# First weight rows by one transfer each on two queues, ordered on VectorE while two more rows land

## The chip, the core and the metric

The kernel runs on one core of a Trainium2 chip. The core has a matrix engine (TensorE), a vector engine (VectorE), a scalar engine (ScalarE), GpSimd and SyncE, and transfers between main memory and the on-chip memory are issued by SyncE and by ScalarE, each through a queue of its own. In the profile these are PE (PEld for TensorE's weight loads), DVE, ACT, POOL and SP; "SPq" and "ACTq" are the instruction streams that issue transfers. The metric is the time of one execution in microseconds (us) on the device.

## What is computed

A weight matrix of 1024 x 1024 is pruned 2 of 4: along its first axis, each group of four consecutive rows keeps, in every column, the elements whose magnitude is at least the second largest of the four. Then 16 x 512 tokens of 1024 features are multiplied by the pruned matrix and a bias is added. All values are bfloat16.

```python
def reference(x, w, b):          # x 16 x 512 x 1024, w 1024 x 1024, b 1024
    B, S, D = x.shape
    N, M = 2, 4
    G = D // M
    wg = w.reshape(G, M, D)
    mag = jnp.abs(wg)
    order = jnp.argsort(mag, 1)
    thr = jnp.take_along_axis(mag, order[:, M - N:M - N + 1, :], 1)
    mask = (mag >= thr).astype(w.dtype)
    wp = (wg * mask).reshape(D, D)
    return jnp.einsum("bsd,df->bsf", x, wp) + b
```

## The kernel before

**Tiling.** The 8192 tokens are 64 tiles of 128. The output's 1024 columns are two halves of 512, one bank of accumulators each. The contraction over 1024 rows is eight steps of 128. A weight tile keeps one group of four rows on one partition: it is 128 partitions (groups) x 4 rows x columns. Two such tiles in the row direction (g = 0, 1) make the matrix.

**Pruning in pieces.** The matrix is pruned in six pieces (L61): four of g = 0, 256 columns wide, two of g = 1, 512 wide. For each, `abs_piece` (L109) takes magnitudes, on VectorE by masking the sign bit (L120) or for piece 3 on ScalarE (L117). `prep_piece` (L124) then forms, on VectorE, the larger (hi, L131) and smaller (lo, L132) of rows 0 and 1 and of rows 2 and 3, both pairs in one instruction; t1 and t2 (L135, L136); the threshold (L138), which is the second largest of the four; the mask (L145) and the product of weights and mask (L148). For piece 0 the magnitudes are taken in two instructions (rows 0 and 1, rows 2 and 3), and so are mask and product, rows 0 and 1 first.

**The start.** Transfers are issued at the top (L83 to L91), in program order on each queue. SyncE: rows 0 and 1 of piece 0's weights (128 KB), token tiles 0 and 1 (256 KB), tile 4 (128 KB), tile 5, the weights of piece 1 (256 KB), tiles 6 and 7, and the weights of pieces 2 and 3 (512 KB). ScalarE: rows 2 and 3 of piece 0's weights, tiles 2 and 3. Then ScalarE loads its function table and makes one small copy (L100). These token loads bring the first half of the features of tiles 0 to 7.

TensorE begins with filler matmuls on a constant (`warm`, L105, 13 of them, 12 before the first transposes; the profile holds records of 12), then transposes token tiles 0 to 3 (L175, four instructions a tile), one more filler, tiles 4 and 5. ScalarE copies each transposed tile out of its bank (L180). Then come the products (L196) of piece 0: for tiles 0, 1, 2 with rows 0 and 1, the same three tiles with rows 2 and 3, tile 3 with all four, tile 4 with rows 0 and 1, then the transposes of tiles 6 and 7 and what is left of piece 0 for the eight tiles; piece 1 follows. The whole order of the start is written out by hand in a string of tokens (`FRONT`), and every engine keeps program order.

**The rest.** Tiles 0 to 13 go through the weights as pieces become ready. Pruned weights are rearranged by transfers on SyncE (`unpack`, L165) into tiles with 128 rows of the contraction on the partitions, and later tokens are brought in already transposed, by transposing transfers on SyncE (L252, L264, L317). From tile 14 on, a loop does 16 matmuls a tile (L364), VectorE adds the bias (L241) and writes an output pair, two tiles to a buffer of 1024 columns each, five buffers in turn. The output of a pair leaves by one transfer of 512 KB on ScalarE's queue (L221), except for pairs in `singly` (L207), where each of the two tiles leaves by a transfer of its own (L214, L217). `singly` holds pairs 10 to 16, that is tiles 20 to 33.

Of the kernel before, what the change touches and what calls it, by code (L numbers as in the profile page):

```python
# [10 lines left out]
def kernel(  # L11
# [7 lines left out]
    nc = tc.nc  # L19
    P = 128  # L20
    bf16 = mybir.dt.bfloat16
    fp32 = mybir.dt.float32
    u16 = mybir.dt.uint16
    Alu = mybir.AluOpType
    Act = mybir.ActivationFunctionType
    K = tc.keep_in_program_order
# [6 lines left out]
    FH = 512  # L33
# [9 lines left out]
    tmp = ctx.enter_context(tc.tile_pool(name="tmp", bufs=2))  # L43
# [21 lines left out]
    def w_of(i):  # L65
        g, c0, c1 = pieces[i]
        return w_gh[(g, c0 // FH)][:, :, c0 % FH:c0 % FH + c1 - c0]

    def load_w(g, c0, c1, eng=nc.sync, m0=0, m1=4):
        dst = w_gh[(g, c0 // FH)][:, m0:m1, c0 % FH:c0 % FH + c1 - c0]  # L70
        K(eng.dma_start(dst, wv[:, g, m0:m1, c0:c1]))
# [4 lines left out]
    def load_x(ta, tb, eng=nc.sync):  # L76
        xt = const.tile([P, tb - ta, KH], bf16, name=f"xh_{ta}")
        src = xf[ta * P:tb * P, 0:KH].rearrange("(t p) c -> p t c", p=P)
        K(eng.dma_start(xt[:], src))
        for t in range(ta, tb):  # L80
            xh[t] = xt[:, t - ta, :]

    load_w(0, 0, 256, nc.sync, 0, 2)  # L83
    load_w(0, 0, 256, nc.scalar, 2, 4)
    load_x(0, 2)
    load_x(2, 4, nc.scalar)
    load_x(4, 5)
    load_x(5, 6)
    load_w(0, 256, 512)
    load_x(6, 8)  # L90
# [15 lines left out]

    mags = {}

    def abs_piece(i, on_act):  # L109
        g, c0, c1 = pieces[i]  # L110
        n = c1 - c0
        if n <= 256:
            mag = mags_pool.tile([P, 4, n], bf16, name="mag")[:]
        else:
            mag = mag2_pool.tile([P, 4, n], bf16, name="mag2")[:]
        if on_act:
            K(nc.scalar.activation(mag, w_of(i), Act.Abs))  # L117
        else:
            for ms in (slice(0, 2), slice(2, 4)) if i == 0 else (slice(0, 4),):
                K(nc.vector.tensor_single_scalar(  # L120
                    mag[:, ms].bitcast(u16), w_of(i)[:, ms].bitcast(u16), 0x7FFF, op=Alu.bitwise_and))
        mags[i] = mag

    def prep_piece(i):  # L124
        g, c0, c1 = pieces[i]
        n = c1 - c0
        mag = mags.pop(i)
        magv = mag.rearrange("p (a j) f -> p a j f", j=2)
        hi = tmp.tile([P, 2, FH], bf16, name="hi")[:, :, :n]
        lo = tmp.tile([P, 2, FH], bf16, name="lo")[:, :, :n]  # L130
        K(nc.vector.tensor_tensor(hi, magv[:, :, 0, :], magv[:, :, 1, :], op=Alu.max))  # L131
        K(nc.vector.tensor_tensor(lo, magv[:, :, 0, :], magv[:, :, 1, :], op=Alu.min))  # L132
        t1 = tmp.tile([P, FH], bf16, name="t1")[:, :n]
        t2 = tmp.tile([P, FH], bf16, name="t2")[:, :n]
        K(nc.vector.tensor_tensor(t1, hi[:, 0, :], hi[:, 1, :], op=Alu.min))  # L135
        K(nc.vector.tensor_tensor(t2, lo[:, 0, :], lo[:, 1, :], op=Alu.max))  # L136
        thr = tmp.tile([P, FH], bf16, name="thr")[:, :n]
        K(nc.vector.tensor_tensor(thr, t1, t2, op=Alu.max))  # L138
        mask = tmp.tile([P, 4, FH], bf16, name="mask")[:, :, :n]

        halves = (slice(0, 2), slice(2, 4)) if i < 3 else (slice(0, 4),)

        def keep(ms):
            tb = thr[:, None, :].to_broadcast([P, ms.stop - ms.start, n])
            K(nc.vector.tensor_tensor(mask[:, ms], mag[:, ms], tb, op=Alu.is_ge))  # L145

        def prune(ms):
            K(nc.vector.tensor_tensor(w_of(i)[:, ms], w_of(i)[:, ms], mask[:, ms], op=Alu.mult))  # L148

        if i == 0:  # L150
            for ms in halves:
                keep(ms)
                prune(ms)
        else:
            for ms in halves:
                keep(ms)
            for ms in halves:
                prune(ms)
# [45 lines left out]
            o_left[t // 2] = 2 if t == NT - 2 else 4  # L204
        return o_pair[t // 2][:, t % 2, :]

    singly = range(10, 17)  # L207

    def half_done(t):
        p = t // 2  # L210
# [82 lines left out]
    for tok in FRONT.split():  # L293
        k, *n = tok.split(".")
        n = [int(c) for c in n]
# [4 lines left out]
        elif k in "Ww":  # L300
            warm(FH if k == "W" else P)
        elif k == "A":
            abs_piece(n[0], n[0] == 3)
        elif k == "P":
            prep_piece(n[0])
        elif k == "T":
            transpose_half(n[0])
# [91 lines left out]
```

## Time and profile before

| | |
|---|---|
| runs (3), us | 233.02, 233.14, 233.35; median 233.14 |
| profiled execution, us | 233.16, of which 231.4 from first to last instruction |
| TensorE | 227.9 us busy, 98% |
| VectorE | 120.4 us busy, 52% |
| ScalarE | 18.0 us busy, 8% |
| main loop's matmuls (L364, 752 on the large token batches) | 162.5 us |
| piece products of g = 0 (L196, 256 columns, 128 of them) | 14.5 us |
| transposes on TensorE (L175) | 32 |

The queue streams at the start, with start and duration in us, the issuing engine, the line, the operation, what is written from what, and how many in a row:

```profile
0.73 0.46 SPq L71 DMA_DIRECT2D w<-in_w_dram  x1
0.74 0.49 ACTq L71 DMA_DIRECT2D w<-in_w_dram  x1
1.25 1.43 SPq L79 DMA_DIRECT2D xh<-in_x_dram  x3
1.26 0.50 ACTq L79 DMA_DIRECT2D xh<-in_x_dram  x1
1.79 1.28 ACT L100 ACT_TABLE_LOAD   x1 [1.79 <-issue]
2.73 0.68 SPq L71 DMA_DIRECT2D w<-in_w_dram  x1
3.44 0.61 SPq L79 DMA_DIRECT2D xh<-in_x_dram  x1
4.10 1.24 SPq L71 DMA_DIRECT2D w<-in_w_dram  x2
```

The duration of an issue is the time on the issuing engine only; how long a transfer takes to land stands in the view of transfers ("us to landing"). Lines of the list of waits read: who waited, for whom, us in total, times, the longest. In the timeline the bracket tells how long the engine was idle before and what ended that. Matmul durations in the profile overlap each other, so TensorE's pace is read from starts, not from durations.

### The profile page before, as it was taken

What the parts mean: (1) busy time and instruction counts of PE and PEld (TensorE: products, weight loads), DVE (VectorE), ACT (ScalarE), POOL (GpSimd) and SP (SyncE); (2) the same over time, 40 slices, a digit from 0 to 9 for tenths busy, and PEclk for the clock granted to TensorE, in tenths of its full rate; (3) what the DMA queues carried; (4) which work ended last, traced back from release to release, by engine and by line L of the source; (5) the groups of instructions that cost most, each with busy time, mean ns of one, the idle gap of its engine ahead of it and who ended that gap; (6) DMA issues with size and microseconds to landing.
All of it is one profiled execution on the core that took longest, in us unless ns stands there. A gap on an engine that the chain in (4) does not pass through costs nothing.

```text
span 231.4 us, 2786 instructions
## 1 busy us (share of the span) xinstructions
PE 227.9 (98%) x1156; PEld 110.8 (48%) x1156; DVE 120.4 (52%) x208; ACT 18.0 (8%) x33; POOL 0.7 (0%) x6
## 2 busy tenths in 40 slices
PE   8999999999999999999999999999999999999995
PEld 4887444444444444444444444444444444444443
DVE  3899887867987424424424424423423433433434
ACT  3777500000000000000000000000000000000000
POOL 1000000000000000000000000000000000000000
PEclk9999999999999999999999999999999999999999
DMA  6989998999957222991259622696129961122222
GB/s 208 264 179 233 218 192 177 267 258 270 320 189 272 91 95 70 235 284 58 81 129 251 164 93 92 137 241 192 68 91 200 224 211 40 53 91 91 91 93 91
DMA packets 77100, 38.19 MB, mean 165 GB/s; under 512 B 63136, under 2 KB 68896, under 8 KB 77088
## 3 DMA queue, kind: packets, MB, share of 16 engines
q1 hardware_dynamic: 67712, 20.91, 44.5%
q10 hardware_dynamic: 9376, 17.11, 20.4%
q8 instruction: 9, 0.15, 0.3%
q14 instruction: 3, 0.02, 0.0%
HBM read 3.41 MB, written 16.78 MB: 87 GB/s over the span
## 4 chain that ended last, share of the span: by engine, by line
PE 98%; DVE 0%; issue 0%
PE bank L364 73%; PE bank L196 17%; PE bank L256 6%; PE bank L105 2%; PE bank L175 1%; DVE o_last L347 0%
## 5 line engine op out<-in xcount | busy, mean ns | idle before, releaser
L364 PE MATMUL bank<-wp_nat,xTb 128*128 128x512 bf16 x752 | 162.5, 379 | 0.0
L241 DVE TENSOR_TENSOR o_pair<-bank,bias_sb 128x512 bf16<-128x512 f32 x104 | 67.3, 686 | 99.5 <-PE bank L364 96.3
L364 PEld LDWEIGHTS <-xTb 128*128 128x128 bf16 x752 | 73.6, 98 | 88.7
L232 DVE TENSOR_TENSOR stage<-bank,stage 128x512 f32<-128x512 f32 x22 | 14.4, 687 | 3.4 <-PE bank L196 3.3
L196 PE MATMUL bank<-w,xT 128*128 128x256 bf16 x128 | 14.5, 273 | 0.0
L196 PE MATMUL bank<-wp_nat,xg 128*128 128x512 bf16 x64 | 14.1, 379 | 0.0
L236 DVE TENSOR_TENSOR o_pair<-stage,bias_sb 128x512 bf16<-128x512 f32 x22 | 14.0, 683 | 0.0
L196 PEld LDWEIGHTS <-xT 128*128 128x128 bf16 x128 | 12.2, 98 | 1.8 <-ACT xT L180 0.2
L228 ACT COPY stage<-bank 128x512 f32<-128x512 f32 x22 | 11.4, 611 | 3.7 <-PE bank L196 3.7
L196 PE MATMUL bank<-wp_nat,xfill 128*128 128x512 bf16 x48 | 10.7, 379 | 0.0
L256 PE MATMUL bank<-wp_nat,xfill 128*128 128x512 bf16 x48 | 10.5, 379 | 0.0
L196 PEld LDWEIGHTS <-xg 128*128 128x128 bf16 x64 | 6.3, 98 | 7.5
L256 PEld LDWEIGHTS <-xfill 128*128 128x128 bf16 x48 | 4.7, 97 | 5.7
L196 PEld LDWEIGHTS <-xfill 128*128 128x128 bf16 x48 | 4.7, 98 | 5.4
L364 PE MATMUL bank<-wp_nat,xTs 128*128 128x512 bf16 x32 | 7.1, 379 | 0.0
L145 DVE TENSOR_TENSOR mask<-mag,thr 128x512 bf16<-128x512 bf16 (+2 forms) x9 | 5.5, 630 | 0.2
L148 DVE TENSOR_TENSOR w<-w,mask 128x512 bf16<-128x512 bf16 (+2 forms) x9 | 5.5, 630 | 0.2
L105 PE MATMUL bank<-const-bfloat16-1.0 128*128 128x512 bf16 (+1 forms) x12 | 4.4, 542 | 0.8 <-PEq L383 0.8
L364 PEld LDWEIGHTS <-xTs 128*128 128x128 bf16 x32 | 3.1, 98 | 3.8
L120 DVE TENSOR_SCALAR mag<-w 128x512 uint16<-128x512 uint16 (+2 forms) x6 | 2.7, 468 | 3.1 <-DMA w<-in_w_dram 3.1
L180 ACT COPY xT<-bank 128x512 bf16<-128x512 bf16 x8 | 4.1, 607 | 2.8 <-PE bank L175 2.8
L256 PE MATMUL bank<-wp_nat,xTb 128*128 128x64 bf16 (+3 forms) x40 | 3.7, 251 | 0.0
(20 smaller groups left out, 26.4 us busy)
## 6 DMA issues: line engine op xcount, KB each, us to landing
out_dram<-o_pair ACTq DMA_DIRECT2D x24, 512.0 KB, 2.8
out_dram<-o_pair ACTq DMA_DIRECT2D x15, 256.0 KB, 2.1
wp_nat<-w SPq DMA_DIRECT2D x16, 128.0 KB, 2.9
w<-in_w_dram SPq DMA_DIRECT2D x3, 512.0 KB, 6.9
xh<-in_x_dram SPq DMA_DIRECT2D x2, 256.0 KB, 4.4
xh<-in_x_dram ACTq DMA_DIRECT2D x1, 256.0 KB, 4.0
xh<-in_x_dram SPq DMA_DIRECT2D x2, 128.0 KB, 3.9
w<-in_w_dram SPq DMA_DIRECT2D x1, 256.0 KB, 4.2
```

What stands on the lines that cost most here:

```text
L105: K(nc.tensor.matmul(bank[7][:, :n], lhsT=ones[:, :P], rhs=ones[:, :n], start=True, stop=True))
L120: K(nc.vector.tensor_single_scalar(mag[:, ms].bitcast(u16), w_of(i)[:, ms].bitcast(u16), 0x7FFF, op=Alu.bitwise_and))
L145: K(nc.vector.tensor_tensor(mask[:, ms], mag[:, ms], tb, op=Alu.is_ge))
L148: K(nc.vector.tensor_tensor(w_of(i)[:, ms], w_of(i)[:, ms], mask[:, ms], op=Alu.mult))
L180: K(nc.scalar.copy(xt[:], src))
L196: K(nc.tensor.matmul(dst, lhsT=lhs, rhs=rhs, start=c0 == 0 and m == 0, stop=c1 == FH and m == 3))
L228: K(nc.scalar.copy(stage[(h, t)][:], bank[own[(h, t)]][:]))
L232: K(nc.vector.tensor_tensor(st, bank[own[(2 + h, t)]][:], st, op=Alu.add))
L236: K(nc.vector.tensor_tensor(get_o(t)[:, f], stage.pop((h, t))[:], bias_sb[:, f], op=Alu.add))
L241: K(nc.vector.tensor_tensor(get_o(t)[:, f], bank[bk][:], bias_sb[:, f], op=Alu.add))
L256: K(nc.tensor.matmul(bank[bk][:, :c1 - c0], lhsT=xN[t][:, kt, :], rhs=wp_nat[h][:, kt, c0:c1], start=kt == 0, stop=kt == KT - 1))
L364: K(nc.tensor.matmul(bank[bks[h]][:], lhsT=xN[t][:, kt, :], rhs=wp_nat[h][:, kt, :], start=kt == 0, stop=kt == KT - 1))
```

## The change

Four things are edited.

- The weights of rows 0 and 1 of piece 0 come by two transfers of 64 KB, row 0 on SyncE's queue and row 1 on ScalarE's, both first on their queues. Rows 2 and 3 (128 KB) are second on SyncE's queue.
- Token tiles 0 and 1 move from SyncE's queue to ScalarE's, tiles 2 and 3 from ScalarE's to SyncE's, tile 4 from SyncE's to ScalarE's.
- For piece 0, hi and lo of a pair of rows are formed directly after that pair's magnitudes, so that VectorE's order is abs, hi, lo of rows 0 and 1, then abs, hi, lo of rows 2 and 3, each hi and lo 256 columns wide instead of 2 x 256. For the other pieces the instructions are as they were.
- `singly` starts at pair 11: the outputs of tiles 20 and 21 leave by one transfer.

```diff
-    load_w(0, 0, 256, nc.sync, 0, 2)
-    load_w(0, 0, 256, nc.scalar, 2, 4)
-    load_x(0, 2)
-    load_x(2, 4, nc.scalar)
-    load_x(4, 5)
+    load_w(0, 0, 256, nc.sync, 0, 1)
+    load_w(0, 0, 256, nc.scalar, 1, 2)
+    load_w(0, 0, 256, nc.sync, 2, 4)
+    load_x(0, 2, nc.scalar)
+    load_x(2, 4)
+    load_x(4, 5, nc.scalar)
     load_x(5, 6)
     load_w(0, 256, 512)
     load_x(6, 8)
...
+    pairs = {}
+
+    def order_pairs(i, mag, a):
+        n = mag.shape[-1]
+        if i not in pairs:
+            pairs[i] = (tmp.tile([P, 2, FH], bf16, name="hi")[:, :, :n], tmp.tile([P, 2, FH], bf16, name="lo")[:, :, :n])
+        magv = mag.rearrange("p (a j) f -> p a j f", j=2)
+        for dst, op in zip(pairs[i], (Alu.max, Alu.min)):
+            K(nc.vector.tensor_tensor(dst[:, a], magv[:, a, 0, :], magv[:, a, 1, :], op=op))
...
-            for ms in (slice(0, 2), slice(2, 4)) if i == 0 else (slice(0, 4),):
+            for a in ((0, 1), (1, 2)) if i == 0 else ((0, 2),):
+                ms = slice(2 * a[0], 2 * a[1])
                 K(nc.vector.tensor_single_scalar(
                     mag[:, ms].bitcast(u16), w_of(i)[:, ms].bitcast(u16), 0x7FFF, op=Alu.bitwise_and))
+                if i == 0:
+                    order_pairs(i, mag, slice(*a))
...
-        magv = mag.rearrange("p (a j) f -> p a j f", j=2)
-        hi = tmp.tile([P, 2, FH], bf16, name="hi")[:, :, :n]
-        lo = tmp.tile([P, 2, FH], bf16, name="lo")[:, :, :n]
-        K(nc.vector.tensor_tensor(hi, magv[:, :, 0, :], magv[:, :, 1, :], op=Alu.max))
-        K(nc.vector.tensor_tensor(lo, magv[:, :, 0, :], magv[:, :, 1, :], op=Alu.min))
+        if i > 0:
+            order_pairs(i, mag, slice(0, 2))
+        hi, lo = pairs.pop(i)
...
-    singly = range(10, 17)
+    singly = range(11, 17)
```

## The prediction, made before the changed kernel had run

> **What bounds the kernel now.** I read the head of the page and its chain of waits first. TensorE is busy for nearly the whole span, and the chain that ends last is TensorE alone.
>
> ```profile
> span 231.4 us, 2786 instructions
> PE 227.9 (98%) x1156; PEld 110.8 (48%) x1156; DVE 120.4 (52%) x208; ACT 18.0 (8%) x33; POOL 0.7 (0%) x6
> PE 98%; DVE 0%; issue 0%
> ```
>
> So the end moves only if TensorE's first 11 us move. Next I read the chain in order of time there, the list of waits, and single instructions in narrow timeline windows.
>
> ```profile
> 0.77 4.21 PE bank L105 x11
> 4.99 1.20 PE bank L175 x16
> ...
> 6.68 2.15 PE bank L196 x18
> 8.84 0.51 PE bank L175 x8
> 9.35 36.21 PE bank L196 x222
> ```
>
> ```profile
> PEld L196 <- ACT xT L180: 0.2, 1, 0.2
> PEld L175 <- DMA xh<-in_x_dram: 0.2, 1, 0.2
> ```
>
> Filler matmuls (L105) run to 4.78, tokens are transposed (L175), and then the products start (L196). The narrow windows show where TensorE waits after 4.78, against matmuls that follow each other in 0.055 us (128 columns) or 0.109 (256): 0.05 at 6.57 (rows 0 and 1 pruned), 0.06 at 7.07 (third copied token tile), 0.07 at 7.37 (rows 2 and 3 pruned), 0.07 around 8.71 (tokens 6 and 7 land), 0.02 at 10.29. In all 0.27 us, 0.12% of the span: no shorter wait at the front can bring more. The fillers also stay, so nothing can start before 4.78.
>
> The third reading is VectorE in its timeline and the transfers by their issue windows.
>
> ```profile
> 3.55 0.53 DVE L120 TENSOR_SCALAR mag<-w 128x512 uint16<-128x512 uint16 x2 [2.68 <-DMA w<-in_w_dram]
> 4.11 0.43 DVE L131 TENSOR_TENSOR hi<-mag 128x512 bf16<-128x512 bf16 x1
> 4.45 0.42 DVE L132 TENSOR_TENSOR lo<-mag 128x512 bf16<-128x512 bf16 x1
> 4.79 0.29 DVE L135 TENSOR_TENSOR t<-hi 128x256 bf16<-128x256 bf16 x1
> 4.99 0.28 DVE L136 TENSOR_TENSOR t<-lo 128x256 bf16<-128x256 bf16 x1
> ```
>
> ```profile
> w<-in_w_dram SPq DMA_DIRECT2D x1, 128.0 KB, 2.8
> w<-in_w_dram ACTq DMA_DIRECT2D x1, 128.0 KB, 3.0
> ...
> xh<-in_x_dram SPq DMA_DIRECT2D x1, 256.0 KB, 3.5
> xh<-in_x_dram ACTq DMA_DIRECT2D x1, 256.0 KB, 4.0
> ```
>
> Issued at 0.73 and 0.74, the two weight halves land at 3.53 and 3.74. Tokens 0 and 1 (SyncE's queue, issued 1.25) land at 4.75, just as the fillers end; tokens 2 and 3 (ScalarE's, 1.26) at 5.26, and are wanted at 5.52.
>
> **The first weight rows.** Rows 0 and 1 become two transfers of 64 KB, and 128 KB fewer lie in front of them. The two queues together move 256 GB/s between 1.9 and 3.3 and about 350 at the end of that stretch, so 128 KB are worth 0.37 to 0.5 us against the later half's 3.74. Bounds for the landing: 3.25 to 3.74 (no gain, if the fixed part of the 3.0 us rules). I take 3.40, nearer the gain, since the bytes ahead are halved in any case.
>
> The Trainium skill speaks against this step: the page "DMA: Bandwidth & Descriptors", section "Issuing engines are not separate DMA queues", says that transfers from several engines share the same DMA engines and that only issue time is saved. The two rows above (2.8 and 3.0 us side by side) agree in that neither queue has the wires to itself. If only that rule counted and the landing stayed at 3.74, the sum below would end 0.35 us later.
>
> **VectorE's share.** The row 3.55 to 4.79 is the old stretch from first weights to t: two abs, one hi, one lo, 1.24 us. The new one has six instructions: abs, hi, lo, abs, hi, lo. The spacings: abs to a hi that needs it 0.33 (the second abs at 3.78 to 4.11); 256-column tensor operations 0.20 apart (4.79 to 4.99). So 0.33 + 0.20 + 0.20 for each half, 1.46 us with no wait. From 3.42 that puts t at 4.88, 0.09 later than 4.79. It breaks even with a landing at 3.31. Rows 2 and 3 must be there when the second abs wants them, at 4.15. They are now second on SyncE's queue beside tokens 0 and 1: no earlier than 3.74 (the same 256 KB end then), and, if all 256 KB of tokens slip in between at 350 GB/s, as late as 4.5. I take 3.95, covered by 0.2 us of VectorE's own work. With that cover gone each further 0.1 costs 0.1. t therefore comes between 4.73 and 5.22, 4.88 taken.
>
> What is queued behind on VectorE: the threshold, masks and products of piece 0, then all of piece 1. TensorE's start at 6.57 and 7.37 goes 0.09 later; 0.035 of that is given back at 8.71, where it waits for tokens 6 and 7 until 8.67 anyway. Piece 1's last product ends at 10.64 and is wanted at 10.74, so a delay of the same 0.05 passes there too. At 11.04 VectorE waits for the next weights by DMA (0.40 us idle), and later pieces are as before. Cost: 0.05 us.
>
> **Tokens 0 and 1 on ScalarE's queue.** Second on that queue, with 64 KB ahead. Between SyncE's 4.75 and ScalarE's old 5.26; the 64 KB that are gone from ahead are 0.2 us at 350 GB/s, so not over 5.06. I take 4.85, 0.10 late, keeping 4.6 (no use, the fillers run) to 5.26. Late by d, the copies on ScalarE (L180, 0.48 apart, the bound until 7.07) start d later; of d, 0.07 is given back where rows 2 and 3 are waited for and 0.035 at 8.71. So 0.10 costs nothing beyond VectorE's 0.05, the two overlapping. Tokens 2 and 3 on SyncE's queue behind more bytes: 5.0 to 5.5, wanted at 5.52, cost 0. Token tile 4 goes from SyncE to ScalarE, wanted at 6.02 with 0.33 us to spare, cost 0; tile 5 stays on SyncE with 64 KB less ahead. ScalarE issues three transfers instead of two, 0.50 each, so its table load ends at 3.58 instead of 3.08; its next work is at 5.45, which hides it. SyncE issues as many before the weights of piece 1 as before (four), so those and tokens 6 and 7 leave at 2.73 and 3.44 again.
>
> **What is not moved but comes near.** Tokens 6 and 7 took 5.2 us from 3.44 and end on the path: bounds -0.2 to +0.5 us (from nothing to the 0.5 that the two queues differ by above). I take 0: they leave at the same time with the same bytes ahead. One more transfer at the front costs its issue on ScalarE, priced above; if SyncE must besides wait for an early landing before it issues so many, the early ones are down by 4 and the large weights leave at 4.10, so that lies within the same upper bound.
>
> **The outputs of tokens 20 and 21.** Two transfers of 256 KB (81.23 and 84.69, 2.1 us each) become one of 512 KB at 84.69, 2.8 us by the paired rows, so it ends at 87.5; SyncE's next transposing load is issued at 90.48 and the output buffer is wanted five pairs later. Cost 0; with that cover gone, 0.7.
>
> **The sum.** +0.05 (VectorE) + 0 (tokens) + 0.02 for one instruction that waits on two landings (half of the 0.05 between a product's end at 7.32 and TensorE's start at 7.37): +0.07 on the profiled execution's own 233.16 (span 231.4 and 1.8 around it), 233.23; the runs' median is 233.14, 0.02 below it, so 233.2.
>
> **Rivals.** (a) First tokens late: on ScalarE's queue they land as that queue's row did, at 5.26 or after. TensorE idles 0.5 us, ScalarE's copies go with it, 0.10 is given back: +0.4, 233.55. For: the row itself. Against: half the bytes ahead. From a landing of 5.35 on it is over 0.2%. Chance 0.15.
>
> (b) Slow TensorE lasts longer. Until 5.5 matmuls start 0.427 apart for 512 columns, later 0.216: the clock doubles after 4.7 us of work. If an empty stretch at 4.78 made that count begin anew, 4.5 us more would run at half speed, +2.2, less the 0.27 of waits that vanish: 235.1. Against: the array is full for the whole 4 us before. Chance 0.08. The Trainium skill, "TensorE: Matmul & The Clock Gate", Part 1, ties the step to a free-running window of 3.4 us of activity; by it the estimate is half of 3.4 us later, less the same waits, 234.6; that page alone has the window, one clock step is all this trace shows.
>
> (c) A tail of the DMA queue: tokens 6 and 7, or the weights of 11.04 (piece 2's pruning ends 0.05 before it is used at 14.2), land 0.5 late because the queues' shares changed. Each 0.1 costs 0.1: 233.7. For: no slack at either. Against: the same bytes lie ahead. Chance 0.12.
>
> (d) Faster: row landings before 3.3, and the waits at 6.57, 7.37 and 8.71 vanish: -0.1 to -0.27, 232.95. Against: needs three landings better at once. Chance 0.13.
>
> (e) The change does not bring the first rows earlier (3.7): VectorE 0.4 late, +0.35; it is the upper end of my forecast, chance 0.52 for that whole case.
>
> **How the numbers follow.** A measurement of this kernel tells 0.2%, 0.47 us. Slower by more: all of (b), half of (a) and of (c), and 0.04 of the forecast's tail, together 0.25. Faster by more needs more than all waits of the front, that is, an earlier clock step: 0.05. The rest, 0.70, is within. Range 233.0 to 233.8: left out are (b), half of (d) and the far end of (c).
>
> **What would show it.** VectorE's first abs near 3.4 and t near 4.9; the first transposes at 4.78 to 4.95; products from 6.6; tokens 6 and 7 again near 8.7; from 11 us on every TensorE start shifted by one constant, under 0.2. An idle TensorE at 4.8 shows (a); 512-column starts or transposes at half speed after 5.5 show (b). The prediction is wrong if a wait after 11 us appears, or if the shift is over 0.4 either way.

## The result, and the profile after

| | before | changed |
|---|---|---|
| median, us | 233.22 (232.86 to 233.88, 12 runs) | 233.63 (233.55 to 233.97, 12 runs) |
| ratio | | 1.0020, 95% interval 1.0011 to 1.0029 |
| profiled execution, us | 233.16 (span 231.4) | 233.62 (span 231.8) |

The changed kernel is slower by 0.2%, some 0.4 to 0.5 us. The head of the page and the chain that ended last, of the changed kernel:

```profile
span 231.8 us, 2769 instructions
PE 227.1 (98%) x1137; PEld 110.9 (48%) x1156; DVE 120.7 (52%) x210; ACT 18.1 (8%) x33; POOL 0.7 (0%) x6
PE 95%; DMA 2%; issue 1%; DVE 0%; SPq 0%
```

Before, the chain was TensorE alone; now 2% of it is a transfer. The same chain in order of time (start, us, what):

```profile
1.19 0.42 SPq L71
1.65 4.55 DMA xh<-in_x_dram
6.24 0.64 PE bank L187 x8
6.94 0.45 PE bank L187 x8
7.38 1.97 PE bank L208 x18
9.35 0.45 PE bank L187 x8
```

The load of token tiles 2 and 3, issued on SyncE's queue at 1.65, takes 4.55 us; only at 6.20 are they there, and TensorE's third transposed tile starts at 6.24. Before, it started at 5.57 (its weight load at 5.52). The same load was issued at 1.26 before, as the second on ScalarE's queue; now it is the third on SyncE's and its issue starts 0.39 us later. The transfers by their issue windows (KB each, us from issue to landing; the one with 5.3 is the weights of piece 1):

```profile
w<-in_w_dram ACTq DMA_DIRECT2D x1, 64.0 KB, 2.3
w<-in_w_dram SPq DMA_DIRECT2D x1, 64.0 KB, 2.1
...
xh<-in_x_dram ACTq DMA_DIRECT2D x1, 256.0 KB, 3.8
w<-in_w_dram SPq DMA_DIRECT2D x1, 128.0 KB, 2.8
...
xh<-in_x_dram SPq DMA_DIRECT2D x1, 256.0 KB, 4.5
xh<-in_x_dram ACTq DMA_DIRECT2D x1, 128.0 KB, 4.4
...
w<-in_w_dram SPq DMA_DIRECT2D x1, 256.0 KB, 5.3
```

Rows 0 and 1 land at 2.83 and 3.00 (3.53 for both together before), rows 2 and 3 at 3.95 (3.76), tiles 0 and 1 at 4.95 (4.74), tiles 2 and 3 at 6.20 (5.24), the weights of piece 1 at 7.93 (6.91), tiles 6 and 7 at 8.62 (8.67). So the first rows come early, and two loads behind them, tiles 2 and 3 and the weights of piece 1, come a microsecond late. Tiles 4 and 5 come 0.4 later too (6.07 and 6.47, before 5.69 and 6.07). VectorE and TensorE in the timeline:

```profile
3.02 0.29 DVE L132 TENSOR_SCALAR mag<-w 128x512 uint16<-128x512 uint16 x1 [2.15 <-DMA w<-in_w_dram]
...
4.71 0.28 DVE L147 TENSOR_TENSOR t<-hi 128x256 bf16<-128x256 bf16 x1
...
6.24 0.64 PE L187 MATMUL bank<-ident,xh 128*128 128x128 bf16 x8 [0.21 <-DMA xh<-in_x_dram]
...
7.22 2.13 PE L208 MATMUL bank<-w,xT 128*128 128x256 bf16 x18
7.96 0.43 DVE L132 TENSOR_SCALAR mag<-w 128x1024 uint16<-128x1024 uint16 x1 [0.71 <-DMA w<-in_w_dram]
```

VectorE reaches t at 4.71 instead of 4.79, and the pruned rows 0 and 1 are there at 6.45. TensorE's first product starts at 7.22 instead of 6.57, 0.65 later: it waits for nothing on VectorE any more. Of the 0.65, 0.20 is given back, since the waits of before at 7.07, 7.37 and 8.71 no longer arise. From the first product behind the transposes of tiles 6 and 7 (9.63, before 9.19) to the end of the span TensorE is shifted by one constant, 0.45 us within 0.01. VectorE sits idle 0.71 us until the weights of piece 1 land, but the first product of piece 1 starts at 11.19, no more than the same 0.45 after the 10.74 of before.

### The profile page after: what moved, and what is told of

Its sections match the earlier page's. It is cut to its first block, busy times and chain, and to the rows that moved or that the text cites. A ratio compares the mean times of both kernels' runs of the same rounds, so it can differ in the third digit from the quotient of the medians.

```text
span 231.8 us, 2769 instructions
## 1 busy us (share of the span) xinstructions
PE 227.1 (98%) x1137; PEld 110.9 (48%) x1156; DVE 120.7 (52%) x210; ACT 18.1 (8%) x33; POOL 0.7 (0%) x6
## 4 chain that ended last, share of the span: by engine, by line
PE 95%; DMA 2%; issue 1%; DVE 0%; SPq 0%
PE bank L376 73%; PE bank L208 16%; PE bank L268 6%; DMA xh<-in_x_dram 2%; PE bank L187 1%; DVE o_last L359 0%; SPq L71 0%; PE bank L106 0%
```

## The experiments

Each kernel was timed against the kernel before on the same chip. "Ratio" is to that, with its 95% interval. Landing times are read from a single trace each.

**The changed kernel once more.** No edit.

> The changed kernel once more, for a second trace. Token theory (TensorE waits until tiles 2 and 3 land on SyncE's queue, 6.2 us in the first trace against 5.2 before): the landing comes again at 6.0 to 6.3, TensorE's third transposed tile starts right behind it, and the time is 233.5 to 233.8. Clock theory (the later doubling of TensorE's clock, at 5.96 us instead of 5.49, is what costs): the doubling is again near 5.96 whenever the time is 0.4 up; if it comes at another moment, the time follows it by half of the difference. Chance theory (one late landing in one execution): tiles 2 and 3 land at 5.3 to 5.6 this time and the time is 233.2.

233.81 us, ratio 1.0028 (1.0017 to 1.0038). TensorE in the timeline of the second trace:

```profile
0.77 3.65 PE L106 MATMUL bank<-const-bfloat16-1.0 128*128 128x512 bf16 x11 [0.77 <-PEq L395]
5.25 0.64 PE L187 MATMUL bank<-ident,xh 128*128 128x128 bf16 x8 [0.84 <-DMA xh<-in_x_dram]
6.33 0.64 PE L187 MATMUL bank<-ident,xh 128*128 128x128 bf16 x8 [0.44 <-DMA xh<-in_x_dram]
```

Tiles 2 and 3 land at 6.28 again: the late landing is no chance. The clock theory falls. The eleven fillers ahead of the transposes took 3.65 us in this trace and 4.21 in the first, because TensorE's pace doubled at 3.7 us here and at 5.96 there, and the profiled executions still took 233.72 and 233.62.

**The outputs of tiles 20 and 21 singly.** Edit on the changed kernel:

```diff
-    singly = range(11, 17)
+    singly = range(10, 17)
```

> The outputs of tiles 20 and 21 by a transfer each again, all else as in the changed kernel. All theories of the start: no change against the changed kernel, 233.6 within 0.1. Output theory (the joined transfer of 512 KB costs): 233.2 to 233.4.

233.88 us, ratio 1.0027 (1.0016 to 1.0037), as the changed kernel beside it. The joined output costs nothing that can be seen; tiles 2 and 3 landed at 6.11 in this trace too.

**VectorE's new order alone.** The kernel before with `order_pairs` for piece 0, all transfers and `singly` as before.

> The kernel before with VectorE's new order alone (six instructions for piece 0 instead of four), all transfers as before. VectorE theory: first weights at 3.53, t at 5.0 instead of 4.79, rows 2 and 3 pruned 0.2 later, of which 0.04 is given back at tokens 6 and 7: 233.3, +0.15. If VectorE's first piece does not bind: 233.15, within 0.05 of before.

233.26 us against 233.09, ratio 1.0003 (0.9994 to 1.0011): no difference. In this trace the two weight halves landed at 3.26 and 3.47, and t started at 4.76, 1.48 us after the first abs could start: the six instructions take what was worked out. Only the first landing differs from the 3.53 that was assumed.

**VectorE's old order on the new transfers.** Edit on the changed kernel:

```diff
-                if i == 0:
-                    order_pairs(i, mag, slice(*a))
...
-        if i > 0:
-            order_pairs(i, mag, slice(0, 2))
+        order_pairs(i, mag, slice(0, 2))
```

> The changed kernel with VectorE's order of before for piece 0 (both abs, then one hi and one lo over both pairs); transfers as in the changed kernel. Arithmetic from the changed kernel's trace: second abs at 3.97, hi at 4.30, lo at 4.64, t at 4.98 instead of 4.71. Wait theory (TensorE waits for tiles 2 and 3 until 6.24, the first product is at 7.2, the pruned rows are there at 6.5): no change against the changed kernel, 233.6 to 233.8. VectorE theory: +0.2, 233.9.

233.75 us, ratio 1.0031 (1.0020 to 1.0042). t starts at 5.34 instead of the 4.98 worked out, for rows 2 and 3 landed at 4.31 this time. Tiles 2 and 3 landed at 5.94, and the first product is at 7.13, directly behind VectorE. The time isn't told apart from the changed kernel's: VectorE's order has little or no weight while tiles 2 and 3 land this late.

**Swapping the token tiles alone.** Edit on the kernel before:

```diff
-    load_x(0, 2)
-    load_x(2, 4, nc.scalar)
+    load_x(0, 2, nc.scalar)
+    load_x(2, 4)
```

> The kernel before with token tiles 0 and 1 on ScalarE's queue and tiles 2 and 3 on SyncE's, nothing else (tile 4 stays on SyncE's). Token theory by queue: each pair lands as its queue's row did before, tiles 0 and 1 at 5.25, tiles 2 and 3 at 4.75; TensorE begins its transposes at 5.3, 0.5 late, and gives 0.1 back: 233.5, +0.4. If the queue does not matter, only the order of issue: tiles 0 and 1 at 4.8 and no change, 233.15.

233.53 us, ratio 1.0019 (1.0010 to 1.0028). The list of waits and TensorE's timeline:

```profile
PEld L175 <- DMA xh<-in_x_dram: 0.7, 1, 0.7
```

```profile
5.44 1.14 PE L175 MATMUL bank<-ident,xh 128*128 128x128 bf16 x16 [0.46 <-DMA xh<-in_x_dram]
```

As the theory by queue said: tiles 0 and 1 land at 5.39 on ScalarE's queue, tiles 2 and 3 at 4.94 on SyncE's. With equal transfers ahead of both, ScalarE's queue is the later one by 0.5 us (before: 4.74 and 5.24, the other way round).

**Token tiles back, weight rows split.** Edit on the changed kernel:

```diff
-    load_x(0, 2, nc.scalar)
-    load_x(2, 4)
-    load_x(4, 5, nc.scalar)
+    load_x(0, 2)
+    load_x(2, 4, nc.scalar)
+    load_x(4, 5)
```

> Token tiles on their old queues (0, 1 and 4 on SyncE's, 2 and 3 on ScalarE's), the weight rows and VectorE's new order as in the changed kernel. Token theory: tiles 2 and 3 land by 5.3, the wait before the third transposed tile is gone; tiles 0 and 1, now behind two weight transfers on SyncE's queue, land at 4.9 to 5.2, and the time is 233.2 to 233.4, at least 0.2 under the changed kernel. Clock theory: no change against the changed kernel, 233.6, as long as TensorE has an empty stretch at 4.8. Rows theory (the three weight transfers at the head push everything behind them back): 233.6, with tiles 0 and 1 after 5.3.

233.79 us, ratio 1.0026 (1.0016 to 1.0037): no gain. The wait has moved. Tiles 2 and 3, second on ScalarE's queue, land at 4.70; tiles 0 and 1, now third on SyncE's, at 5.42; and tiles 6 and 7, with one more load ahead of them on SyncE's queue and issued 0.4 later, at 9.33 instead of 8.67, which TensorE waits for.

**Weight rows back, token tiles swapped.** Edit on the changed kernel:

```diff
-    load_w(0, 0, 256, nc.sync, 0, 1)
-    load_w(0, 0, 256, nc.scalar, 1, 2)
-    load_w(0, 0, 256, nc.sync, 2, 4)
+    load_w(0, 0, 256, nc.sync, 0, 2)
+    load_w(0, 0, 256, nc.scalar, 2, 4)
```

> The weight rows by two transfers again (rows 0 and 1 on SyncE's queue, rows 2 and 3 on ScalarE's); token tiles swapped and VectorE's new order as in the changed kernel. Token theory: tiles 2 and 3, now behind 128 KB instead of 192 KB on SyncE's queue, land at 5.4 to 5.9; tiles 0 and 1, behind 128 KB on ScalarE's queue, at 5.1 to 5.3; time 233.3 to 233.6. Rows theory: the time is that of before, 233.2. VectorE theory (the six instructions instead of four cost): t starts 0.2 later than before with the first landing at 3.5, and the time is 233.3 to 233.4.

233.69 us, ratio 1.0020 (1.0011 to 1.0029). Tiles 2 and 3, second on SyncE's queue again, land at 4.93 instead of 6.20, earlier than expected; tiles 0 and 1 at 5.38 on ScalarE's, as in the swap alone, and TensorE waits for these. The time lies just above the 233.3 to 233.6 expected. t at 4.76 (first landing 3.27) binds nothing, so the 0.2 of the VectorE theory didn't come.

**Rows 2 and 3 on ScalarE's queue.** The split rows, with this head:

```diff
-    load_w(0, 0, 256, nc.sync, 2, 4)
-    load_x(0, 2, nc.scalar)
-    load_x(2, 4)
-    load_x(4, 5, nc.scalar)
+    load_w(0, 0, 256, nc.scalar, 2, 4)
+    load_x(0, 2)
+    load_x(2, 4, nc.scalar)
+    load_x(4, 5)
```

> Rows 0 and 1 by a transfer each as in the changed kernel, but rows 2 and 3 on ScalarE's queue, and all token tiles on their queues of before; VectorE's new order. Queue theory (what lies ahead on a queue, in rows of transfers, sets the landing): on SyncE's queue 128 rows fewer than before, so tiles 0 and 1 by 4.5, tokens 6 and 7 by 8.0; on ScalarE's 128 more, so tiles 2 and 3 at 5.7 to 6.0, wanted at 5.5, some 0.2 to 0.4 late, and the time is 233.3 to 233.5. If the loads share one pace whatever the queue: tiles 2 and 3 near 5.3 and 233.1.

234.01 us, ratio 1.0039 (1.0026 to 1.0051), worse than either theory said. Its loads of rows 2 and 3 and of tiles 2 and 3, and TensorE:

```profile
w<-in_w_dram ACTq DMA_DIRECT2D x1, 128.0 KB, 3.7
xh<-in_x_dram ACTq DMA_DIRECT2D x1, 256.0 KB, 4.9
```

```profile
6.58 0.64 PE L187 MATMUL bank<-ident,xh 128*128 128x128 bf16 x8 [0.74 <-DMA xh<-in_x_dram]
```

Tiles 2 and 3 are third on ScalarE's queue and land at 6.53. Rows 2 and 3, behind row 1 on the same queue, come at 4.89 instead of 3.95. The queue that carries two weight transfers ahead of a token pair pays, whichever queue it is.

**Tiles 2 and 3 ahead of rows 2 and 3.** The changed kernel with these two loads on SyncE's queue in the other order:

```diff
-    load_w(0, 0, 256, nc.sync, 2, 4)
-    load_x(0, 2, nc.scalar)
     load_x(2, 4)
+    load_x(0, 2, nc.scalar)
+    load_w(0, 0, 256, nc.sync, 2, 4)
```

> The changed kernel with the token tiles 2 and 3 issued before rows 2 and 3 of the weights on SyncE's queue, so second on it instead of third. Place theory (each queue lands its transfers in order and the third in line is 0.7 to 1.3 us later than the second): tiles 2 and 3 land at 4.6 to 5.2 instead of 6.2, rows 2 and 3 at 5.0 to 5.6 instead of 4.0; VectorE's second half then starts at 5.0 to 5.6, the first product at 7.5 to 8.1, and the time is 233.9 to 234.6. Bytes theory (tiles 2 and 3 land late because more bytes go over both queues before them): tiles 2 and 3 stay at 5.8 to 6.2.

235.16 us, ratio 1.0091 (1.0076 to 1.0106). The second and third loads on SyncE's queue, VectorE's second abs, and TensorE's first product:

```profile
xh<-in_x_dram SPq DMA_DIRECT2D x1, 256.0 KB, 3.4
w<-in_w_dram SPq DMA_DIRECT2D x1, 128.0 KB, 4.2
```

```profile
5.88 0.30 DVE L132 TENSOR_SCALAR mag<-w 128x512 uint16<-128x512 uint16 x1 [2.05 <-DMA w<-in_w_dram]
```

```profile
8.40 2.26 PE L208 MATMUL bank<-w,xT 128*128 128x256 bf16 x18 [1.86 <-DVE w L160]
```

Second in line, tiles 2 and 3 land at 4.59 instead of 6.20; third in line, rows 2 and 3 land at 5.85 instead of 3.95, later than the 5.0 to 5.6 expected, and the time is above the 233.9 to 234.6 expected too. The bytes theory falls: the same loads go over both queues, and their order on one queue decides who is late. The weights of piece 1, issued at 2.67 as in the changed kernel, landed at 7.02 here instead of 7.93. VectorE's second half, and with it TensorE's first product, wait for rows 2 and 3 to land.

**A third queue.** Rows 2 and 3 issued by GpSimd, tokens on their queues of before:

```diff
-    load_w(0, 0, 256, nc.sync, 2, 4)
-    load_x(0, 2, nc.scalar)
-    load_x(2, 4)
-    load_x(4, 5, nc.scalar)
+    load_w(0, 0, 256, nc.gpsimd, 2, 4)
+    load_x(0, 2)
+    load_x(2, 4, nc.scalar)
+    load_x(4, 5)
```

> Rows 0 and 1 by a transfer each on SyncE's and ScalarE's queues as in the changed kernel, rows 2 and 3 by GpSimd, the token tiles on their queues of before and second there; VectorE's new order. Place theory: tiles 0 and 1 by 4.6, tiles 2 and 3 by 5.2, tokens 6 and 7 by 8.6; if rows 2 and 3 land by 4.0, t is at 4.75 or earlier and the time is 233.0 to 233.15, at best 0.15 under before; if they land at 5, t comes at 5.8 and the time is 233.9. Bytes theory: tiles 2 and 3 as late as in the changed kernel, 6.0 to 6.3, and 233.6.

234.61 us, ratio 1.0067 (1.0055 to 1.0079). The load by GpSimd:

```profile
w<-in_w_dram POOLq DMA_DIRECT2D x1, 128.0 KB, 4.2
```

The token pairs land at 4.61 and 4.94, both earlier than before (4.74 and 5.24), each second in line. But GpSimd's 128 KB take 4.2 us and land at 5.45, where the other two queues need 2.7 to 3.7 for the same load in second place. Rows 2 and 3 are then 1.5 late, t comes at 6.21 and the first product at 7.99.

**Without the wait for tiles 2 and 3.** The load stays; the transposes read other data, so the products of tiles 2 and 3 are not the reference's. Edit on the changed kernel:

```diff
-        xv = xh[t].rearrange("p (q m) -> p m q", m=4)
+        xv = xh[t - 2 if t in (2, 3) else t].rearrange("p (q m) -> p m q", m=4)
```

> The changed kernel with the transposes of token tiles 2 and 3 reading the data of tiles 0 and 1, so that TensorE doesn't wait for the load of tiles 2 and 3, which still runs; the output rows of tiles 2 and 3 are those of tiles 0 and 1 for half of the features. If the wait for tiles 2 and 3 alone makes the 0.45 us: TensorE's third tile starts at 5.6 to 5.9, the first product near 6.7, and the time is 233.2. If another late landing takes its place (the weights of piece 1, 7.9 against 6.9, behind which VectorE's piece 1 ends at 11.0 and is then wanted at 10.7): the first product is early, but the first product of piece 1 still starts at 11.1 and the time stays 233.5 to 233.6.

233.48 us against 233.09, ratio 1.0016 (1.0005 to 1.0026); the runs spread from 232.96 to 234.25. In the trace (233.33 us) the first product is at 6.85, and VectorE then waits for piece 1:

```profile
7.73 0.43 DVE L132 TENSOR_SCALAR mag<-w 128x1024 uint16<-128x1024 uint16 x1 [0.42 <-DMA w<-in_w_dram]
```

Piece 1's first product starts at 10.86, directly behind VectorE, against 10.74 before and 11.19 in the changed kernel. Neither expectation held as it stood: the other late landing does take over, but at 0.1, as the load came at 7.70 this time.

**Without either wait.** As in the last experiment, and the magnitudes of piece 1 are taken of piece 0, so that which weights of piece 1 are kept differs from the reference too. Further edit:

```diff
-                    mag[:, ms].bitcast(u16), w_of(i)[:, ms].bitcast(u16), 0x7FFF, op=Alu.bitwise_and))
+                    mag[:, ms].bitcast(u16), w_of(0 if i == 1 else i)[:, ms].bitcast(u16), 0x7FFF, op=Alu.bitwise_and))
```

> As the kernel without the wait for tiles 2 and 3 (their transposes read tiles 0 and 1), and the magnitudes of piece 1 are taken of piece 0's weights, so that VectorE doesn't wait for the load of piece 1 either; which weights of piece 1 are kept and the products of tiles 2 and 3 differ from the reference. Two-landings theory (tiles 2 and 3 at 6.2, then the weights of piece 1 at 7.7 to 8.0, make the whole): VectorE starts piece 1 at 7.2 to 7.3 instead of 7.7 to 8.0, the first product of piece 1 is at 10.6 to 10.75, TensorE runs from there within 0.1 of the kernel before, and the time is 233.1 to 233.3. If tiles 0 and 1, 0.2 late, cost besides: 0.1 to 0.2 more, 233.3 to 233.5. If something else is behind the 0.4: 233.5 or more.

In the trace VectorE starts piece 1 at 7.43, its first product is at 10.78, and TensorE is 0.04 behind the kernel before from there on; the profiled execution took 233.25 (233.16 before). Over the repeated runs, however, the median is 233.47 against 233.09, ratio 1.0013 (1.0005 to 1.0022), and the profiled execution was the second fastest of the twelve. The trace thus falls under the two-landings theory and the median under the case that tiles 0 and 1 cost besides. The median is 0.38 us above the kernel before, where the kernels with the changed head and both waits were 0.41 to 0.73 above it (the changed kernel twice, single outputs, old order). In the repeated runs taking both waits away is worth between 0.03 and 0.35 us, and the intervals overlap: half of the difference or more stays.

## Why the prediction was right, and where it was not

**The bound and the sign.** TensorE's first 11 us set the end, a shift made there stays constant to the end, and no gain was to be had there: all as predicted. The time lies in the range, and within 0.2% was the likeliest outcome; the ratio of 1.0020 stands at that edge. The size was wrong: +0.07 us was forecast, and +0.4 to +0.7 was measured in the two timings of the changed kernel, the second of which, 233.81, lies just above the range. By the prediction's own last sentence a shift over 0.4 counts against it, and the shift is 0.45 in the first trace and 0.53 in the second. That 233.63 lies in the range is partly luck: the upper part of the range was there for rivals (a), (e) and part of (c), while the load that TensorE waited for was priced at 0.

**The step that failed** is "Tokens 2 and 3 on SyncE's queue behind more bytes: 5.0 to 5.5, wanted at 5.52, cost 0". They landed at 5.9 to 6.3 in all six traces with this head, 0.7 too late in the first (6.20), and with the 0.20 given back that makes the 0.45. The step priced the bytes ahead alone. The load was issued 0.39 later than before, and it was third in its queue. By 3.0 us SyncE's queue had moved 0.18 MB, nearly all of the 192 KB ahead of tiles 2 and 3. Then it almost stood still, as the packets, MB and busy share of the two queues between 3.0 and 3.75 us show (q1 is SyncE's, q10 ScalarE's). Before:

```profile
q1 hardware_dynamic: 196, 0.20, 75.0%
q10 hardware_dynamic: 115, 0.08, 33.2%
```

Changed:

```profile
q10 hardware_dynamic: 163, 0.16, 80.3%
q1 hardware_dynamic: 52, 0.03, 11.8%
```

With tiles 2 and 3 second instead, such a gap came from 3.75 to 4.25 (52 packets), when SyncE's queue had moved 0.31 MB, nearly all of its first two loads. Why the queue pauses isn't shown. Second on either queue, token pairs landed at 4.6 to 5.4 (before, token swap, rows back, tiles 2 and 3 ahead, GpSimd). Third, behind two weight transfers, they landed at 5.4 (tiles 0 and 1 with the tokens back), 5.9 to 6.3 (the changed head) and 6.5 (rows 2 and 3 on ScalarE's queue). Splitting one weight transfer made five loads for the two queues where there had been four, so one of the five that TensorE or VectorE wants first had to be third.

How much of this is the place itself is not fully separated: third in line also meant an issue 0.4 later and 64 KB or more besides on the same queue. Where only the bytes differ, a token pair second behind 64 KB instead of 128 KB landed at 4.6 to 4.7 instead of 4.6 to 4.9 on SyncE's queue, and at 4.7 to 5.2 instead of 5.1 to 5.4 on ScalarE's. So 64 KB are worth some tenths of a microsecond, less than the 1.0 or more between second place on SyncE's queue (4.6 to 4.9) and the changed head (5.9 to 6.3). Nor does the place alone fix the time: third on SyncE's queue, issued at 1.65 behind the same loads, a pair landed at 5.42 when tile 4 came behind it on the same queue, and at 5.9 to 6.3 when tile 4 was on ScalarE's. The Trainium skill, page "DMA: Bandwidth & Descriptors", section "Queues, rings and completion order", says that each DMA engine takes turns between the queues and serves each queue in order; the trace agrees in that exchanging two loads on one queue exchanged their landings (6.20 and 3.95 became 4.59 and 5.85).

**The weights of piece 1** were said to leave SyncE as before, and no price was set on their landing. They left at 2.67 and landed at 7.9 instead of 6.9, though the loads issued before them have the same bytes in all. That is the mechanism of rival (c), a tail of the queue, with another load than the two named there. In the changed kernel it lies beside the wait for tiles 2 and 3. With rows 2 and 3 and tiles 2 and 3 exchanged, and all else as in the changed kernel, these weights landed at 7.02, so their delay, too, hangs on the order on SyncE's queue and not on bytes.

**VectorE's share.** The arithmetic held (1.46 us worked out; 1.48 in the order alone), the landing did not: 3.00 instead of 3.40. Rows 2 and 3 landed at 3.95, as taken, but VectorE now wanted them at 3.76, so 0.2 of the gain went into waiting for them. So t came 0.08 earlier than before, not 0.09 later. Part of this is the trace the sum started from: with the old weight transfers the first half landed at 3.53 there, but at 3.26, 3.27 and 3.38 in three other traces with the same two transfers first. One landing time from one execution carries up to 0.27 us of spread, as much as all the waits that were being weighed.

**Tiles 0 and 1** were put at 4.85 and came at 4.8 to 5.2. On ScalarE's queue behind the full 128 KB they would have cost what rival (a) said: the token swap alone gave a landing of 5.39 and +0.4.

**The clock, rival (b).** The doubling of TensorE's pace came at 3.7, 5.5, 6.0 and 6.8 us in four traces (the second of the changed kernel, before, the first of the changed kernel, rows back) with the first filler at 0.77 in all of them, and none came near the 9.3 that a count begun anew at 4.78 would give. The Trainium skill, "TensorE: Matmul & The Clock Gate", Part 1, calls the window of that gate free-running; these moments agree with that, but they spread over 3.1 us, where the page gives the change 500 ns either way.

**Tiles 6 and 7** were taken at 0 and landed 0.05 earlier than before; that says little, for with the transfers of before they landed at 8.67 in one trace and at 7.46 in another. **Tile 4** had 0.33 us to spare and landed 0.38 later, so its cover was gone; TensorE reached it only at 6.77, and it cost nothing there. **The outputs** cost 0, as said.

**What stays open.** In single traces the account nearly closes: the profiled executions took 233.62 with both late loads, 233.33 without the wait for tiles 2 and 3, 233.25 without either, 233.16 before. In the repeated runs the last two differ by 0.4 rather than 0.1 us, so the two waits are shown as the cause in the traced executions and not in the medians. Other loads with this head were later than with the transfers of before as well: tiles 0 and 1 by up to 0.6 (4.78 to 5.21 against 4.62 and 4.74), rows 2 and 3 by up to 0.8 (3.95 to 4.31 against 3.47 and 3.76), tiles 4 and 5 by up to 0.7. How much of this shows may depend on when TensorE's pace doubles; whether it is the rest wasn't tried. Nor is it known why SyncE's queue pauses. No arrangement that was run is faster than the kernel before.

## What to carry to other kernels

At the head of a kernel, price a load by what its place in the queue brings (a later issue, a pause of the queue, the bytes ahead) and not by the bytes alone: here a token pair second in line landed at 4.6 to 5.4 us and third at 5.4 to 6.5. Splitting a transfer brings its first part early and pushes the loads next behind it back by a place, so the gain (0.5 us on the first weights here) must be on the path, and the loads that lose a place must have that much slack. Where the waits to be saved add up to 0.27 us, look at several traces of the old kernel first: the first landings alone spread by 0.1 to 0.3, and that of tiles 6 and 7 by 1.2.

## What the runs showed of the hardware

- With 128 KB ahead on each, the second load on ScalarE's queue landed 0.45 to 0.5 us after the second on SyncE's, though both were issued within 0.01 us (4.74 and 5.24; with the tiles exchanged 4.94 and 5.39). With 64 KB ahead on each it was 0.28 and 0.33 (4.59 and 4.87; 4.61 and 4.94).
- First on its queue, a load of 64 KB landed 2.1 to 2.3 us after its issue beside another of its size, one of 128 KB 2.5 to 3.0.
- Between 3.0 and 3.75 us SyncE's queue moved 0.03 MB in the changed kernel and 0.20 before, and the two queues together 0.19 and 0.28.
- 128 KB issued by GpSimd took 4.2 us while SyncE's and ScalarE's queues carried loads of their own.
- The moment at which TensorE's pace doubles moved between 3.7 and 6.8 us from trace to trace.
